# Three edits in the expert layers of an attention and two-MoE kernel: row masks first, 116-partition loads cut in two, two loads freed from a wait

## The chip, the cores and the metric

One core of a Trainium2 chip. The metric is the device time of one execution in microseconds (us). The kernel before was timed three times: median 1523.1 us, from 1520.05 to 1523.97. One further execution was profiled; the rows below come from it.

## What is computed

Attention without softmax over 4 sequences of 2496 tokens, then two expert layers (MoE) on the 9984 rows that come out. Cut to what matters:

```python
scores = scale * z @ z.T                      # per sequence
x = u * (maximum(scores, 0) ** 2 @ v)         # 9984 x 256
# first layer: only rows with x @ w_skip > 0; one expert of 8 per row
xc = x[x @ w_skip > 0]
e_idx = argmax(xc @ w_gate)
y[e_idx == e] = gate_w * (maximum(xc @ w1[e], 0) @ w2[e])
out = x;  out[chosen] = xc + y
# second layer: all rows, logits = x @ w_gate + modality_bias[modality_id]
out2[e_idx == e] = gate_w * (maximum(x @ w1[e], 0) @ w2[e])
```

Everything is float32; a product is made of three matmuls of a high and a low part (hh, hl, ...).

## The kernel before, in words

Attention writes its rows, sorted by expert, into two lists in DRAM: `rows1` (rows that the first layer computes) and `rows2` (rows that go straight to the second layer). The class `Moe1` works through `rows1` in tiles of 348 rows, held as 116 partitions x 3 rows (`P1, G1 = 116, 3`); `Moe2` through `rows2` in tiles of 512 rows, 128 partitions x 4. One tile is one *turn* (`turn`, with the lists `PLAN` that say what is done after which step): eight `hidden(f)` steps ("h", 0 to 7), eight `out_part(f)` steps ("o", 0 to 7). Between them hooks are called in the written order; the order on every engine is the order of the program (`manual_schedule`).

What a turn of Moe1 does beside its matmuls:

- "next", at the start: SyncE (SP) reads the next tile's row and expert, loads its rows into `x_in` (`load_rows`, line 758) and the first weights into `w1raw` (line 667). "load w2" follows at ("h", 5). Loads wait in SP's queue, in order.
- "after", eleven times: the gating of the tile computed in the turn before, as a list of steps: `taken` (ScalarE copies the outputs out of PSUM, lines 896 and 897), `low(0)`, `low(1)` with `masks` (lines 933 to 938, six small VectorE operations; `counted` is lines 790 and 791), `logits_t`, `logits` (line 926 reads `x_cur`), `first` (FirstMax, lines 115 to 121), `sums`, `exp`, `rows(0)`, `rows(2)` with `close`, `ranks`. `close` also loads the turn's own rows a second time, into `x_cur`.
- "w2": ScalarE makes the high part of the second weights, GpSimd (POOL) the low part with `TENSOR_TENSOR` (line 678), two of them for each of four blocks. "w1": ScalarE and VectorE (line 680).
- `send`: POOL scatters the rows of the last tile into `rows2`, three indirect DMAs (line 694) with small touches between (line 716).

In the order of VectorE `masks` stands between `low(1)` and the third `hl` (line 783), which frees a PSUM buffer that `hidden` needs (`ps_h` has three).

Turns in order: one inside the tail of attention, two with rows that are known, a loop (line 1206) over the table's tiles, one behind the loop in which Moe2's first tile (`ra`, of the expert with most rows) is loaded, one with Moe2's second known tile (`rb`), then Moe2's own turns and loop (line 1235). A loop ends with a meeting of all engines (shown at line 1296). `ra` and `rb` are registers that SP loads; those two tiles are full of rows that attention itself has written, if the expert has so many, and rows past the end are dropped by index.

Tile, the layer that places waits, lets a load from `rows2` wait for all scatters to `rows2` that come before it in the program, unless they are declared independent.

Of the kernel before, what the change touches and what calls it, by code (L numbers as in the profile page):

```python
# [104 lines left out]
class FirstMax:  # L105


    def __init__(self, nc, pool, k, lg, P, n, tag):
        self.nc = nc
        sh = [P, n, E]  # L110
        t = lambda name, *sh: pool.tile([128, *sh], F32, name=name + tag)[:P]
        mx, self.df, self.hot = t("mx", n), t("df", n, E), t("hot", n, E)
        self.ex, self.sm = t("ex", n, E), t("sm", n)
        df, hot = self.df, self.hot
        nc.vector.tensor_reduce(mx, lg, axis=AX.X, op=ALU.max)
        nc.vector.tensor_tensor(df, lg, mx.unsqueeze(2).to_broadcast(sh), op=ALU.subtract)
        nc.vector.scalar_tensor_tensor(
            hot, df, 0.0, k.desc[:P].unsqueeze(1).to_broadcast(sh), op0=ALU.is_equal, op1=ALU.mult
        )
        nc.vector.tensor_reduce(mx, hot, axis=AX.X, op=ALU.max)  # L120
        nc.vector.tensor_tensor(hot, hot, mx.unsqueeze(2).to_broadcast(sh), op=ALU.is_equal)
# [69 lines left out]
class Attention:  # L191
# [148 lines left out]
    def tail(self, b, c):  # L340
# [76 lines left out]
        for g in range(4):  # L417
            yield
            for s, (lst, w) in enumerate(((self.rows1, RW), (self.rows2, C_B2))):
                scatter(self.tc, f"list{s}", lst, ix[:, s, g:g + 1], r[:, g, 0:w])  # L420
# [208 lines left out]
class Shared:  # L629
# [35 lines left out]
    def load(self, i, e):  # L665
        w = self.w[e:e + 1] if isinstance(e, int) else self.w[ds(e, 1)]
        self.nc.sync.dma_start(self.raw[i], w.rearrange("o p w -> p (o w)")[:, i * 2048:(i + 1) * 2048])
# [21 lines left out]
        return self.hi[1][f // 2][:, f % 2], self.lo[1][f // 2][:, f % 2]  # L689


def scatter(tc, key, out, ix, rows, loop=False):

    i = tc.nc.gpsimd.indirect_dma_start(  # L694
        out=out, out_offset=bass.IndirectOffsetOnAxis(ap=ix, axis=0), in_=rows, in_offset=None,
        bounds_check=out.shape[0] - 1, oob_is_err=False,
    )
    i = getattr(i, "ins", i)
    tc.add_to_no_dep_group(key, i)
    tc.declare_no_dep(i, group=key, across_iterations=loop, reason="each row is written once")  # L700


class Scatter:
# [22 lines left out]
    def group(self, out, rows, width, g):  # L726
        last = rows[:, g, width - 1:width]
        self.touch(self.spare, last, last)
        scatter(self.tc, self.key, out, self.ix[:self.P, g:g + 1], rows[:, g, 0:width], True)
# [7 lines left out]
class Moe:  # L737
# [17 lines left out]

    def load_rows(self, r, dst=None):
        src = self.rows[r:r + self.T] if isinstance(r, int) else self.rows[ds(r, self.T)]
        self.nc.sync.dma_start(self.x_in if dst is None else dst, src.rearrange("(p g) w -> p g w", g=self.G))

    def x_transposed(self, d, ps=None, x=None):  # L760

        nc = self.nc
        ps = (self.sh.ps_x.tile([128, 512], F32, name="m") if ps is None else ps)[:, :self.T]
        for g in range(self.G):
            nc.tensor.transpose(  # L765
                ps[:, g * self.P:(g + 1) * self.P], (self.x_in if x is None else x)[:, g, d * 128:(d + 1) * 128],
                self.k.ident[:self.P, :self.P],
            )
        nc.scalar.copy(self.xh[:, d], ps)  # L769
        nc.vector.tensor_tensor(self.xl[:, d], ps, self.xh[:, d].bitcast(F32), op=ALU.subtract)  # L770
# [35 lines left out]
    def turn(self, follow, after, hooks=None):  # L806

        nc, sh = self.nc, self.sh
        nxt = []

        def hook(what, *args):
            if what == "next":
                nxt.extend(follow())
                nxt[0].load_rows(nxt[2])
                sh.load(0, nxt[1])
            elif what == "after":
                next(after, None)
            elif what == "w2":
                sh.split(1, args[0], nc.gpsimd)
            elif what == "w1":  # L820
                sh.split(0, args[0], nc.vector)
            elif what == "x":
                nxt[0].x_transposed(args[0])
            elif what == "load w2":
                sh.load(1, nxt[1])
            else:
                what()

        plan = self.PLAN if hooks is None else hooks
        for h in plan["start"]:  # L830
            hook(*h)
        self.work({at: [lambda h=h: hook(*h) for h in hs] for at, hs in plan.items()})
        for _ in after:
            pass


class Moe1(Moe):
# [45 lines left out]
    def after(self, lim, current, ps=None, gate_first=True):  # L883

        nc, k, P, G, T = self.nc, self.k, self.P, self.G, self.T
        s, sh = self.p, self.sh
# [12 lines left out]
        def low(d):  # L899
            nc.vector.tensor_tensor(yl[:, d], y[:, d], yh[:, d].bitcast(F32), op=ALU.subtract)  # L900
# [74 lines left out]

        both = lambda *f: lambda: [i() for i in f]
        exp = lambda: gate["first"].exp()
        begin = [taken, lambda: low(0), both(lambda: low(1), masks), logits_t]
        if gate_first:
            steps = begin + [logits, first, sums, exp, lambda: rows(0), both(lambda: rows(2), close), ranks]  # L980
        else:
# [16 lines left out]
class Moe2(Moe):  # L998
# [12 lines left out]

    def __init__(self, sh, k, rows, out):
        super().__init__(sh, k, rows, C_B2, P2, G2)
        self.out = out

    def more(self, p):
        super().more(p, "2")
# [4 lines left out]
    def take_y(self):  # L1022

        self.y = self.sh.y + [self.sh.ps_m.tile([128, 2 * D], F32, name="m") for _ in range(2)]

    def x_transposed(self, d):
        if d == 0:
# [61 lines left out]
def forward_kernel(ctx, tc, zT, v, uT, wg, wg2, mod, bias, w, out, nb=B, mode="reg_based"):  # L1089
# [33 lines left out]
    m2 = Moe2(sh, k, rows2, out)  # L1123
    spare = lambda: sh.ps_m.tile([128, 512], F32, name="m")
    nc.gpsimd.memset(sh.x_in, 0.0)
    with ExitStack() as main:
        a = Attention(tc, sh, ctx, main, k, zT, v, uT, wg, rows1, rows2, carry, nb)
# [7 lines left out]
        known = const.tile([128, 2, E], F32, name="known")  # L1135
# [73 lines left out]
    m1.send()  # L1209
    load = lambda i, lo, hi: nc.values_load(plan.er[0:1, i:i + 1], engines=[SP], min_val=lo, max_val=hi)  # L1210
    e2, ra, rb = load(0, E, 2 * E - 1), load(1, 0, E * N - T2), load(2, 0, E * N - T2)
    m1.turn(lambda: (m2, e2, ra), m1.finish(n))

    m1.send()
# [85 lines left out]
```

## Time and profile before

| | us |
|---|---|
| median of 3 runs | 1523.1 (1520.05 to 1523.97) |
| profiled execution | 1526.42 |
| its span, first to last instruction | 1524.5 |
| TensorE busy | 1477.5 (97%) |
| VectorE / ScalarE / GpSimd busy | 1091.3 / 944.6 / 610.2 |
| granted TensorE clock, mean | 0.995 |

Attention takes the span's first 734 us, Moe1's turns run from there to about 1079, Moe2's to the end. A row of the timeline reads: start, duration, engine, line, operation, output<-input, shape, count, and in brackets the idle time of the engine before it with what ended that. In the views PE is TensorE, DVE VectorE, ACT ScalarE, SP SyncE; a q behind the name is the engine's queue. An indirect DMA on POOL shows the time that POOL spends on it, not the transfer.

### The profile page before, as it was taken

The page shows a single profiled execution, that of the slowest core. Times are in us where ns is not written, and L with a number is a line of the kernel's source. Part 1 is how long each engine was busy: PE and PEld are TensorE (multiplying, and loading weights), DVE is VectorE, ACT ScalarE, POOL GpSimd, SP SyncE. Part 2 cuts the span into 40 slices and gives each one's busy share as a digit, 9 for nine tenths or more (in the row PEclk, how much of TensorE's full clock was granted, in tenths as well). Part 3 has the DMA queues.
Part 4 walks back from the last instruction along what each step waited for, and adds up shares of the span by engine and source line. Part 5 has one row for each costly group of instructions (what it writes and reads, how often), then busy time and mean ns, then how long its engine had stood idle before and what let it go on. Part 6 is the DMA issues. An engine that isn't in the chain of part 4 may idle for free. (4 is left out here: it accounts for less than half of the span.)

```text
span 1524.5 us, 35306 instructions
## 1 busy us (share of the span) xinstructions
PE 1477.5 (97%) x11020; PEld 1271.9 (83%) x11020; DVE 1091.3 (72%) x2587; ACT 944.6 (62%) x1713; POOL 610.2 (40%) x865
## 2 busy tenths in 40 slices
PE   7999999999999999999899999998999999999998
PEld 5888888788887887888789899997888888888886
DVE  7788887888877888787787778886655555555553
ACT  7777777777777777676445555555455455455453
POOL 3022322233322232222455555655454454454454
PEclk9999999999999999999999999999999999999999
DMA  9011211112111140011245555554343433443440
GB/s 365 23 43 63 71 36 42 42 57 76 38 44 53 48 143 28 30 41 62 86 128 165 162 167 164 170 170 141 130 155 124 153 136 124 142 143 127 140 146 27
DMA packets 49701, 160.29 MB, mean 105 GB/s; under 512 B 13285, under 2 KB 15195, under 8 KB 40384
## 3 DMA queue, kind: packets, MB, share of 16 engines
q1 hardware_dynamic: 28720, 124.24, 25.2%
q0 software_dynamic: 20736, 34.71, 6.5%
q8 instruction: 61, 1.00, 0.3%
q14 instruction: 40, 0.33, 0.1%
q10 hardware_dynamic: 144, 0.02, 0.0%
HBM read 124.24 MB, written 46.55 MB: 112 GB/s over the span
## 5 line engine op out<-in xcount | busy, mean ns | idle before, releaser
L694 POOL DMA_INDIRECT rows<-r,ix x160 | 199.4, 1246 | 332.4 <-DVE xs L347 238.2
L334 PE MATMUL o<-ah,vh 64*128 64x512 f32 (+1 forms) x1560 | 311.3, 386 | 9.5 <-DVE xs L347 9.5
L334 PE MATMUL o<-al,vh 64*128 64x512 f32 (+1 forms) x1560 | 303.0, 383 | 0.0
L334 PE MATMUL o<-ah,vl 64*128 64x512 f32 (+1 forms) x1560 | 301.6, 383 | 0.0
L783 DVE SCALAR_TENSOR_TENSOR hl<-ph,hh 128x512 fp32r<-128x512 f32 (+1 forms) x288 | 179.8, 674 | 164.0 <-ACT hh L782 160.9
L678 POOL TENSOR_TENSOR w<-w2raw,w 128x256 fp32r<-128x256 f32 x282 | 199.3, 743 | 181.5 <-issue 161.3
L291 ACT ACTIVATE t<-s 128x1024 f32<-128x1024 f32 (+2 forms) x201 | 202.3, 1007 | 95.7 <-PE s L288 90.2
L305 DVE TENSOR_TENSOR al<-t,ah 128x1024 fp32r<-128x1024 f32 (+2 forms) x201 | 240.0, 1194 | 18.3 <-PE s L288 0.5
L782 ACT ACTIVATE hh<-ph 128x512 fp32r<-128x512 f32 (+1 forms) x288 | 155.9, 541 | 130.7 <-PE ph L780 120.5
L780 PE MATMUL ph<-mxh,zA 128*128 128x512 f32 (+1 forms) x576 | 211.6, 367 | 11.4 <-DVE mlg L926 5.6
L303 ACT ACTIVATE t<-t 128x1024 f32<-128x1024 f32 (+2 forms) x201 | 208.1, 1036 | 5.8
L304 DVE CAST ah<-t 128x1024 fp32r<-128x1024 f32 (+2 forms) x201 | 137.4, 684 | 102.8 <-ACT t L303 63.4
L780 PE MATMUL ph<-mxl,zA 128*128 128x512 f32 (+1 forms) x576 | 208.8, 363 | 0.8 <-DVE mxl L770 0.8
L780 PE MATMUL ph<-mxh,zB 128*128 128x512 f32 (+1 forms) x576 | 208.6, 362 | 0.0
L334 PEld LDWEIGHTS o<-ah,vh 64*128 64x128 f32 x1560 | 150.4, 185 | 45.7 <-DVE xs L347 17.0
L334 PEld LDWEIGHTS o<-al,vh 64*128 64x128 f32 x1560 | 150.3, 185 | 27.3
L334 PEld LDWEIGHTS o<-ah,vl 64*128 64x128 f32 x1560 | 146.7, 185 | 27.4
L769 ACT CAST mxh<-m 128x512 fp32r<-128x512 f32 (+1 forms) x72 | 37.9, 526 | 168.4 <-PE m L765 103.3
L780 PEld LDWEIGHTS ph<-mxh,zA 128*128 128x128 f32 x576 | 109.7, 190 | 27.8 <-DVE mlg L926 5.8
L881 PE MATMUL o<-hh,w 128*128 128x348 f32 x512 | 128.7, 334 | 0.0
L288 PE MATMUL s<-zA,zB 64*128 64x512 f32 (+1 forms) x400 | 124.5, 389 | 0.0
L288 PE MATMUL s<-zB,zA 64*128 64x512 f32 (+1 forms) x400 | 122.1, 389 | 0.0
(236 smaller groups left out, 3070.9 us busy)
## 6 DMA issues: line engine op xcount, KB each, us to landing
w1raw<-in_w SPq DMA_DIRECT2D x36, 1024.0 KB, 6.7
w2raw<-in_w SPq DMA_DIRECT2D x36, 1024.0 KB
x_in<-rows SPq DMA_DIRECT2D x20, 520.0 KB
vraw<-in_v SPq DMA_DIRECT2D x20, 512.0 KB
ut<-in_uT SPq DMA_DIRECT2D x20, 512.0 KB
x_cur<-rows SPq DMA_DIRECT2D x16, 364.3 KB
x_in<-rows SPq DMA_DIRECT2D x15, 364.3 KB
rows<-x_in POOLq DMA_DIRECT2D x8, 536.0 KB
```

Source lines behind the costliest of these rows:

```text
L288: nc.tensor.matmul(s[:, i, :n], w[p, k], x[p, q], start=(j == 0), stop=(j == 2))
L291: nc.scalar.activation(t[:, i, :n], s[:, i, :n], AF.Relu, scale=SCALE)
L303: nc.scalar.activation(t[:, i, :n], t[:, i, :n], AF.Square)
L304: nc.vector.tensor_copy(h[:, i, :n], t[:, i, :n])
L305: nc.vector.tensor_tensor(l[:, i, :n], t[:, i, :n], h[:, i, :n].bitcast(F32), op=ALU.subtract)
L334: nc.tensor.matmul(o[half][d][:, :n], w[p, d * 128:d * 128 + 128], x[p, :n], start=(u == 0 and j == at[0]), stop=(u == 9 and j == at[-1]),)
L678: lo_engine.tensor_tensor(l[:, c], src[:, c], h[:, c].bitcast(F32), op=ALU.subtract)
L694: i = tc.nc.gpsimd.indirect_dma_start(out=out, out_offset=bass.IndirectOffsetOnAxis(ap=ix, axis=0), in_=rows, in_offset=None, bounds_check ...
L780: nc.tensor.matmul(ps, w, x, start=(i == 0), stop=(i == len(mms) - 1))
L782: nc.scalar.activation(h, ps, AF.Relu)
L783: nc.vector.scalar_tensor_tensor(l, ps, 0.0, h.bitcast(F32), op0=ALU.max, op1=ALU.subtract)
L881: nc.tensor.matmul(self.y[d], w[:, dd], h[f], start=(f == 0 and i == 0), stop=(f == 7 and i == 2))
```

## The change

1. `masks` leaves the third step of "after" and is put ahead of `taken` in the first, at the turn's start.
2. `load_rows` issues two transfers where the number of partitions isn't a multiple of 16: 112 partitions and 4 for Moe1's 116; Moe2's 128 stay one transfer. This goes for `x_in`, `x_two` and `x_cur`.
3. Moe2's loads of `ra` and `rb` are declared independent of the scatters of Moe1 ("scatter1"), and those scatters of the loads.

```diff
+def independent(tc, key, other, i, loop, reason):
+    tc.add_to_no_dep_group(key, i)
+    tc.declare_no_dep(i, group=other, across_iterations=loop, reason=reason)
 def scatter(tc, key, out, ix, rows, loop=False):
     i = getattr(i, "ins", i)
-    tc.add_to_no_dep_group(key, i)
-    tc.declare_no_dep(i, group=key, across_iterations=loop, reason="each row is written once")
+    independent(tc, key, key, i, loop, "each row is written once")
+    if loop:
+        tc.declare_no_dep(i, group="loads2", across_iterations=True, reason="rows behind those of full tiles")
 ...
     def load_rows(self, r, dst=None):
         src = self.rows[r:r + self.T] if isinstance(r, int) else self.rows[ds(r, self.T)]
-        self.nc.sync.dma_start(self.x_in if dst is None else dst, src.rearrange("(p g) w -> p g w", g=self.G))
+        dst = self.x_in if dst is None else dst
+        src = src.rearrange("(p g) w -> p g w", g=self.G)
+        most = self.P // 16 * 16
+        return [
+            self.nc.sync.dma_start(dst[p], src[p]).ins
+            for p in (slice(0, most), slice(most, self.P)) if p.start < p.stop
+        ]
 ...
-        begin = [taken, lambda: low(0), both(lambda: low(1), masks), logits_t]
+        begin = [both(masks, taken), lambda: low(0), lambda: low(1), logits_t]
 ...                                   # class Moe2
-        self.out = out
+        self.out, self.known = out, ()
+    def load_rows(self, r, dst=None):
+        for i in super().load_rows(r, dst):
+            if any(r is known for known in self.known):
+                independent(self.tc, "loads2", "scatter1", i, True, "a full tile's rows are there, others are dropped")
 ...                                   # forward_kernel, behind the first loop
+    m2.known = ra, rb
```

## Rows read from the trace of the kernel before

**Rows 1.** The page, part 1: busy time and share of the span, instructions.
```profile
PE 1477.5 (97%) x11020; PEld 1271.9 (83%) x11020; DVE 1091.3 (72%) x2587; ACT 944.6 (62%) x1713; POOL 610.2 (40%) x865
```

**Rows 2.** Waits of TensorE, whole span: us in total, times, longest.
```profile
PE ph L780 <- DVE mlg L926: 5.6, 2, 3.0
...
PE ph L780 <- PEq L1296: 2.6, 2, 1.9
PE m L956 <- DVE x_out L917: 2.0, 2, 1.7
PE ph L780 <- DVE hl L783: 1.6, 6, 0.3
PE m L765 <- DMA x_in<-rows: 1.6, 1, 1.6
```

**Rows 3.** Windows from one turn's first copy (line 896) to the next's; clock behind POOL.
```profile
839.29:857.98 18.69, 18.34 (x123) 17.62 (x122) 15.37 (x46) 10.66 (x24) 11.17 (x18) 1.00 0.57 169
857.98:881.72 23.74, 20.74 (x123) 20.30 (x122) 17.25 (x46) 10.67 (x24) 12.22 (x19) 0.86 0.46 138
...
937.04:955.02 17.98, 17.98 (x123) 17.63 (x122) 14.40 (x46) 10.67 (x25) 11.36 (x18) 1.00 0.58 179
...
801.28:821.31 20.03, 18.32 (x121) 17.58 (x122) 16.18 (x46) 10.88 (x24) 12.09 (x21) 1.00 0.54 155
778.57:801.28 22.71, 20.04 (x124) 19.30 (x122) 16.37 (x46) 10.67 (x25) 10.08 (x14) 0.92 0.52 159
```

**Rows 4.** Windows just behind the two longest waits; granted clock behind POOL's count.
```profile
787.70:791.10 3.40, 3.40 (x13) 3.40 (x13) 1.00 (x3) 0.97 (x2) 0.85 (x2) 0.50 0.28 101
...
866.20:873.00 6.80, 5.82 (x20) 5.82 (x21) 3.72 (x16) 1.47 (x4) 2.41 (x5) 0.50 0.06 20
```

**Rows 5.** Timeline of VectorE at the begin of the turn at 857.98.
```profile
856.64 1.29 DVE L680 TENSOR_TENSOR zB<-w1raw,zA 128x512 fp32r<-128x512 f32 x2
859.89 0.52 DVE L783 SCALAR_TENSOR_TENSOR hl<-ph,hh 128x348 fp32r<-128x348 f32 x1 [1.96 <-ACT hh L782]
...
862.37 4.70 DVE L936 TENSOR_SCALAR mk_drop<-mk 116x3 f32<-116x3 f32 x1
```

**Rows 6.** Timeline of GpSimd in the same stretch.
```profile
857.29 1.80 POOL L694 DMA_INDIRECT rows<-x_out,ix_scatter  x1 [0.53 <-issue]
...
861.34 1.54 POOL L694 DMA_INDIRECT rows<-x_out,ix_scatter  x1 [0.19 <-issue]
862.90 4.15 POOL L678 TENSOR_TENSOR w<-w2raw,w 128x256 fp32r<-128x256 f32 x6
```

**Rows 7.** Timeline of VectorE, the masks of another turn (at 881.72), first and last.
```profile
885.40 0.16 DVE L934 COPY limits<-lim 128x2 f32 x1
...
886.23 0.06 DVE L938 MEMSET cumb<- 116x4 uint32 x1
```

**Rows 8.** Line 936 and tile dfb: duration in ns, least/median/most, of all turns.
```profile
L936 DVE TENSOR_SCALAR mk_drop<-mk x16: 169/637/4703, 764.5 to 1057.8; 116x3 f32<-116x3 f32 x16
...
L116 DVE TENSOR_TENSOR dfb<-mlg,mxb x16: 182/706/2334, 768.2 to 1066.9; 116x24 f32<-116x24 f32 x16
```

**Rows 9.** Windows with one load alone (`x_cur`, then Moe2's `x_in`); last columns DMA share, GB/s.
```profile
1025.90:1029.40 3.50, 3.46 (x23) 3.15 (x21) 2.95 (x9) 1.49 (x3) 0.00 (x0) 1.00 0.24 86
1042.00:1043.50 1.50, 0.80 (x7) 0.52 (x5) 1.40 (x6) 0.01 (x1) 1.11 (x3) 1.00 0.98 329
```

**Rows 10.** Waits of SP's queue from 1024 to 1034: total, times, longest.
```profile
SPq L758 <- DMA rows<-x_out,ix_scatter: 7.3, 1, 7.3
...
SPq L1206 <- DMA x_cur<-rows: 1.5, 1, 1.5
```

**Rows 11.** Timeline of TensorE where the first loop ends.
```profile
1031.28 0.40 PE L780 MATMUL ph<-mxh,zA 128*128 128x348 f32 x1 [1.92 <-PEq L1296]
```

**Rows 12.** Timeline of SP: the loads behind the loop's last turn.
```profile
1024.84 0.30 SPq L758 DMA_DIRECT2D x_cur<-rows  x1
1040.58 0.35 SPq L758 DMA_DIRECT2D x_in<-rows  x1
```

## The prediction, made before the kernel was run

> **What bounds the kernel now.** I began with the page's busy shares: TensorE is busy 97% of the span [rows 1]. So only what shortens TensorE's 47 us of idle time, or speeds its matmuls, can pay. The next view is who TensorE waited for [rows 2]. Five of its waits lie in the stage that the change touches: 5.6 us for `mlg` in two waits, the longer 3.0; 2.6 us in two meetings at loop ends, the longer 1.9, so 0.7 for the other; 2.0 us for `x_out`, most of it one wait of 1.7; 1.6 us for `hl`, six waits of about 0.27; and 1.6 us for one `x_in` load. Together 13.4 us. The rest of the list lies in attention or in the hand-over to it.
>
> The third view cuts Moe1's stage into turns [rows 3]. It shows more than the waits do. Undisturbed turns take 17.98 us (the loop has four, 17.96 to 17.98); the six with the short `hl` wait take 18.7 (five of them 18.66 to 18.71, the sixth is the loop's last); the turns with the long `mlg` waits take 23.74 and 22.71, the first loop turn 20.03. In the two longest, the granted clock means 0.86 and 0.92 instead of 1.00. The fourth view looks just behind their waits: clock 0.50, that is 1.2 instead of 2.4 GHz, for 6.8 us and 3.4 us, after TensorE had stood idle for 3.0 and 2.6 us [rows 4]. So a long wait is paid twice.
>
> Why does `mlg` come late? Not for its data: in the slow turn VectorE is inside `mk_drop`, a 116x3 operation, for 4.70 us [rows 5]. In other turns it takes 0.17 us; the median is 0.64 [rows 8]. It starts at 862.37, while GpSimd works on a scatter (861.34, 1.54 us), and ends at 867.07, as GpSimd's six back-to-back subtractions end (862.90 + 4.15 = 867.05) [rows 6]. VectorE is in order, so three `hl` and `mlg` stand behind it. I read this as one shared way to SBUF which VectorE loses to GpSimd several times in a row.
>
> **Part 1, masks first.** It removes six small VectorE operations from between `low(1)` and the third `hl` and puts them behind the last `zB` of the turn before. No instruction is added. What goes, against the profiled execution (1526.42 us):
> - The turn at 857.98: 23.74 - 17.98 = 5.8 us [rows 3].
> - The turn at 778.57 isn't of the loop's form, so I take its wait and its clock: 5.6 - 3.0 = 2.6 us of waiting [rows 2], and 3.4 us at half the clock, which cost 1.7 [rows 4]. Together 4.3.
> - Six turns at 18.7: at most 18.69 - 17.98 = 0.7 each, 4.2 together [rows 3]; at least the 1.6 us of waits for `hl` [rows 2]. The difference of turns counts all of it, but the later `dfb` may keep a part: I take 0.6 each, 3.6.
> - The first loop turn, 20.03 - 17.98 = 2.05 us [rows 3], is a hold of `dfb` (2.33 us, its longest) by the same GpSimd subtractions [rows 8]. `dfb` isn't moved: I take 0, with 2.05 as the other end.
>
> What it costs: unheld, the six take 885.40 to 886.29, so 0.9 us [rows 7]. At the turn's start VectorE stands idle 1.96 us before the first `hl`, waiting for ScalarE [rows 5]; that covers them. If that cover is gone, the first `hl` is late. At that time GpSimd is on its first scatter: 857.29 + 1.80 = 859.09 [rows 6]. Masks held until then end at 859.09 + 0.9 = 859.99, against 859.89 for `hl` [rows 5], 0.1 us late. I take 0. The other end is a TensorE wait as for today's late `hl`, 0.27 us in each of some 14 turns, 3.8 us [rows 2]. `taken` is on ScalarE and isn't queued behind the masks. What is queued behind them on VectorE: the first `hl` and `low(0)`. POOL's scatters may be held by the masks in turn, by less than the 0.9 us.
>
> Here a page of the Trainium skill says something else. "SBUF — State Buffer", section "SBUF: two separate sides", states that VectorE and GpSimd share a pair of ports, which the one that starts first holds for its whole instruction while the other is blocked. By that rule a small operation waits for one instruction, not for six; the 4.70 us [rows 6] would need another cause, and the two long waits might stay. That is a rival below.
>
> **Part 2, loads in two.** The 116-partition load of `x_cur`, alone on the DMA engines, keeps 0.24 of the 16 busy, some four, at 86 GB/s; Moe2's 128-partition load 0.98 at 329 GB/s [rows 9]. So 112 partitions should go over many more engines, and land sooner. In the loop no TensorE wait names `x_cur`, and the `x_in` wait is behind the loop [rows 2]: no gain there. At the loop's end there is one: the meeting waits 1.5 us of SP's time for `x_cur` to land [rows 10], and TensorE stands idle 1.92 us [rows 11]. The meeting of Moe2's loop, where no such load is under way, costs 0.7 us [rows 2]: 1.9 - 0.7 = 1.2 us gained. The cost is one more issue of 0.3 us on SP per load [rows 12], moved ahead of the load of `w1raw`, for which no TensorE wait is seen [rows 2]; I take 0. Ends: a loss of 0.3 us in the one turn whose `x_in` is waited for, and no gain at all.
>
> The skill has a rule against this edit: "DMA: Bandwidth & Descriptors", section "Rules for kernel authors", says not to bother with two transfers to separate partitions, since both run over the same 16 engines. Its section "Why a DMA increments its semaphore by 16 and not by 1" has the number of engines as the largest divisor up to 16, which is 4 for 116 and 16 for 112; the trace's 0.24 agrees with that one. By the first alone the 1.2 us would not come.
>
> **Part 3, known tiles.** Behind the loop SP waits 7.3 us for scatters [rows 10] before it issues `x_in` at 1040.58 [rows 12]; TensorE then waits 1.6 us for it [rows 2]. Issued 7 us sooner, the load is hidden: 1.6 us gained. `w1raw` stands behind it in SP's queue and comes sooner too. For `rb` no TensorE wait is seen: 0. The end below is that it collides with scatters; I know no row that prices that above the 1.6.
>
> **Sum.** 5.8 + 4.3 + 3.6 + 1.2 + 1.6 = 16.5 us; 1526.4 - 16.5 = 1509.9 in a profiled execution. That execution is 3.3 us above the median of the runs shown. Either profiling costs that, or it met a long hold that the median run missed (one is worth 4.3 to 5.8). I take half, 1.5 us: **1508.5 us**. With all upper ends (4.2 for 3.6, 2.05 for 0, 3.3 for 1.5) it is 1504; with the lower ends (1.6 for 3.6, late `hl` 3.8, a loss of 0.3 for the gain of 1.2) 1515.7.
>
> **Rivals.**
> - *The holds move.* `dfb`, with two SBUF inputs, stays in GpSimd's stream. The shift in phase lets it be held in more turns, at 2.05 us each. For: it happened once in 16, and phases decide. Against: its median is 0.7 us. Four turns: 16.5 - 8.2 = 8.3 gained, 1516.5.
> - *The long holds stay or weren't in the timed runs.* `mk_drop` then waits for something other than the subtractions, which comes along to its new place, or the median run has no long hold to lose. The page's rule above points to the first. Left are 3.6 + 1.2 + 1.6 = 6.4 from the median: 1516.7. Against: both long holds are on `mk_drop`.
> - *The loads don't do what they should*, neither faster nor freed: 2.8 less, 1511.3.
> - *Slower.* The masks at the start hold the scatters' descriptors, GpSimd's subtractions start late in every turn as in the first loop turn, and `dfb` is held each time: 13 x 2.05 = 26.7, less 16.5: 10 us slower, 1535. It decides from 8 turns on (16.5 / 2.05). Against: one turn of 16 does it.
>
> **Chances.** Forecast 0.56, moved holds 0.16, long holds stay 0.13, loads do nothing 0.08, slower 0.07. The range 1503 to 1519 leaves out the slower case and the tails of the second and third, under 0.2. A difference under 0.3% (4.6 us) can't be told from none. Faster by more: 0.56 + 0.08 + 0.12 + 0.08 = 0.84; within: 0.09; slower 0.07.
>
> **What would show it.** Right: `mk_drop` nowhere over about 1 us and ahead of the first `hl`; no wait for `mlg`; all loop turns near 18.0; clock 1.00 in them; the first loop's meeting near 0.7; DMA share near 1 for Moe1's loads; `x_in` behind the loop issued some 7 us sooner, with no TensorE wait. Wrong: `dfb` or another small operation with times over 2 us in several turns, the first `hl` late at the turns' start, or a clock of 0.50 in a new place.

## The result, and the profile of the changed kernel

| | before | changed |
|---|---|---|
| median of 5 runs each, same chip | 1522.75 us (1520.05 to 1523.97) | 1508.45 us (1507.55 to 1509.91) |
| ratio, 95% interval | | 0.9909 (0.9898 to 0.9921) |
| profiled execution, time | 1526.42 us | 1509.91 us |
| profiled execution, span | 1524.5 us | 1507.8 us |

The change saves 14.3 us in the medians and 16.5 us between the two profiled executions. It was forecast at 1508.5 us, from a sum of 16.5 us.

The page of the changed kernel, part 1 (engine, busy us, share of the span, instructions), has the same counts as [rows 1]. The work is the same, and TensorE's share rises from 97% to 98%:

```profile
PE 1471.7 (98%) x11020; PEld 1268.7 (84%) x11020; DVE 1082.8 (72%) x2587; ACT 949.7 (63%) x1713; POOL 614.7 (41%) x865
```

Waits of TensorE over the whole span of the changed kernel (us in total, times, longest). The new lines 969, 793, 930 and 1315 are 956, 780, 917 and 1296 of before:

```profile
PE m L969 <- DVE x_out L930: 3.8, 4, 1.6
PE m L154 <- DVE cuma L140: 2.5, 1, 2.5
...
PE ph L793 <- PEq L1315: 1.4, 2, 0.7
```

Against [rows 2], `mlg` (5.6), `hl` (1.6) and `x_in` (1.6) are gone from the list, and the two meetings are 0.7 each. `x_out` has grown from 2.0 to 3.8.

Windows of the changed kernel: the second turn with known rows ("the second turn" from here on), the loop's first turn, its third, an ordinary one, its fourth, which took 23.74 before, the turn behind the loop, and a stretch in the turn inside attention's tail. Columns: length, busy time of TensorE, its weight loads, VectorE, ScalarE and GpSimd, granted clock, DMA share, GB/s:

```profile
778.70:797.05 18.35, 18.32 (x124) 17.67 (x122) 14.19 (x44) 10.59 (x24) 9.83 (x14) 1.00 0.60 192
797.05:817.00 19.95, 18.29 (x121) 17.64 (x122) 15.95 (x46) 10.84 (x24) 11.88 (x21) 1.00 0.49 161
834.99:852.94 17.95, 17.95 (x123) 17.58 (x122) 14.15 (x47) 10.65 (x24) 11.16 (x18) 1.00 0.55 175
852.94:871.91 18.97, 18.20 (x123) 17.56 (x122) 15.18 (x47) 10.77 (x24) 11.43 (x18) 1.00 0.52 168
1016.60:1036.55 19.95, 18.41 (x122) 17.67 (x123) 15.15 (x47) 10.97 (x24) 12.20 (x21) 1.00 0.57 182
750.50:757.30 6.80, 6.50 (x29) 6.21 (x30) 6.29 (x28) 0.66 (x2) 0.72 (x1) 0.50 0.62 219
```

The second turn falls from 22.71 to 18.35. The turn that took 23.74, the loop's fourth, falls to 18.97 and not to an undisturbed 17.95: its long hold is gone, but another operation is now held in it (below). Five of the six turns at 18.7 are at 17.95; the sixth, the last loop turn, takes 18.99 with the meeting in it (20.92 before). The loop's twelve turns together fall from 230.02 to 219.55 us. In these turns the clock is 1.00; the two half-clock stretches of [rows 4] are gone. The only one left in this stage lies ahead of them, in the turn inside attention's tail, behind the 2.5 us wait for `cuma`. There it lasts 6.8 us; in the kernel before a wait of 3.2 us for `cuma` was followed by 3.4 us of it. The turn behind that one, the first with known rows, is 0.3 us longer (19.41 to 19.71).

Two groups of VectorE in the changed kernel, duration in ns (least/median/most) over all turns:

```profile
L949 DVE TENSOR_SCALAR mk_drop<-mk x16: 169/373/503, 760.2 to 1037.9; 116x3 f32<-116x3 f32 x16
...
L116 DVE TENSOR_TENSOR dfb<-mlg,mxb x16: 182/184/2306, 767.8 to 1051.3; 116x24 f32<-116x24 f32 x16
```

Against [rows 8], `mk_drop`'s longest falls from 4703 to 503 ns. `dfb` still has a longest of 2.3 us, and now three turns have such a hold: 2.31 us in the first loop turn (as before), 1.93 in the loop's fourth turn, at 852.94, and 2.10 in the one behind the loop. The turn at 852.94 shows what holds it. VectorE first, then GpSimd, each as start, duration, line, operation, tiles:

```profile
861.58 1.93 DVE L116 TENSOR_TENSOR dfb<-mlg,mxb 116x24 f32<-116x24 f32 x1
```

```profile
856.21 1.62 POOL L700 DMA_INDIRECT rows<-x_out,ix_scatter  x1 [0.19 <-issue]
857.86 5.60 POOL L678 TENSOR_TENSOR w<-w2raw,w 128x256 fp32r<-128x256 f32 x8
```

`dfb` ends at 863.51, the subtractions at 863.46: the picture of [rows 5] and [rows 6] with another victim.

But not every small operation in the stream is held. The loop's third turn, an ordinary one, VectorE and then GpSimd:

```profile
843.62 0.18 DVE L116 TENSOR_TENSOR dfb<-mlg,mxb 116x24 f32<-116x24 f32 x1
```

```profile
838.07 1.26 POOL L700 DMA_INDIRECT rows<-x_out,ix_scatter  x1 [0.18 <-issue]
839.50 5.63 POOL L678 TENSOR_TENSOR w<-w2raw,w 128x256 fp32r<-128x256 f32 x8 [0.17 <-issue]
```

Here the subtractions run from 839.50 to 845.13, and `dfb` passes among them in its least time. What lets an operation pass isn't shown; the two turns differ in when the subtractions start, 4.5 and 4.9 us behind the turn's begin.

The masks in their new place, VectorE at an ordinary turn's start in the changed kernel:

```profile
942.33 1.28 DVE L680 TENSOR_TENSOR zB<-w1raw,zA 128x512 fp32r<-128x512 f32 x2
943.57 0.06 DVE L946 MEMSET mk_drop<- 116x3 f32 x1
...
944.67 0.06 DVE L951 MEMSET cumb<- 116x4 uint32 x1
945.65 0.52 DVE L796 SCALAR_TENSOR_TENSOR hl<-ph,hh 128x348 fp32r<-128x348 f32 x1 [0.92 <-ACT hh L795]
```

Six operations take 1.2 us from first to last (0.9 unheld [rows 7]), and 0.92 us of VectorE's idle time is left behind them: the cover was enough.

The loop's end in the changed kernel: TensorE at the meeting, then SP's issues behind it, then a window with the load of `x_cur` alone (last columns: clock, DMA share, GB/s):

```profile
1016.57 0.40 PE L793 MATMUL ph<-mxh,zA 128*128 128x348 f32 x1 [0.73 <-PEq L1315]
```

```profile
1018.68 0.36 SPq L769 DMA_DIRECT2D x_in<-rows  x1
1019.28 0.35 SPq L667 DMA_DIRECT2D w1raw<-in_w  x1
```

```profile
1012.30:1013.50 1.20, 1.20 (x11) 1.18 (x10) 1.02 (x6) 0.40 (x2) 0.00 (x0) 1.00 0.81 298
```

The meeting's wait falls from 1.92 [rows 11] to 0.73. `x_in` is issued 2.1 us behind the meeting's matmul instead of 9.3 [rows 11, 12]. The DMA share of the load rises from 0.24 to 0.81 [rows 9].

### The profile page after: what moved, and what is told of

Its sections match the earlier page's. It is cut to its first block, busy times and chain, and to the rows that moved or that the text cites. A ratio compares the mean times of both kernels' runs of the same rounds, so it can differ in the third digit from the quotient of the medians.

```text
span 1507.8 us, 35395 instructions
## 1 busy us (share of the span) xinstructions
PE 1471.7 (98%) x11020; PEld 1268.7 (84%) x11020; DVE 1082.8 (72%) x2587; ACT 949.7 (63%) x1713; POOL 614.7 (41%) x865
## 5 line engine op out<-in xcount | busy, mean ns | idle before, releaser
L700 POOL DMA_INDIRECT rows<-r,ix x160 | 205.5, 1285 | 339.0 <-DVE xs L347 244.5
L796 DVE SCALAR_TENSOR_TENSOR hl<-ph,hh 128x512 fp32r<-128x512 f32 (+1 forms) x288 | 176.5, 614 | 156.7 <-ACT hh L795 156.0
L793 PEld LDWEIGHTS ph<-mxh,zA 128*128 128x128 f32 x576 | 108.4, 188 | 19.6 <-issue 3.7
```

Source lines behind the costliest of these rows:

```text
L700: i = tc.nc.gpsimd.indirect_dma_start(out=out, out_offset=bass.IndirectOffsetOnAxis(ap=ix, axis=0), in_=rows, in_offset=None, bounds_check ...
L793: nc.tensor.matmul(ps, w, x, start=(i == 0), stop=(i == len(mms) - 1))
L796: nc.vector.scalar_tensor_tensor(l, ps, 0.0, h.bitcast(F32), op0=ALU.max, op1=ALU.subtract)
```

## The experiments

The theory has three parts. A VectorE operation is held by GpSimd's stream of subtractions for as long as that runs; 116 partitions go over four DMA engines; and SP waits needlessly behind the loop. The rivals: the masks wait for something else, the holds only move, and the loads are no faster in two transfers.

### The parts alone

**Part 1 alone**, on the kernel before:

```diff
-        begin = [taken, lambda: low(0), both(lambda: low(1), masks), logits_t]
+        begin = [both(masks, taken), lambda: low(0), lambda: low(1), logits_t]
```

> Part 1 alone: the kernel before with the masks at the turn's start, loads and waits as before. Theory (the parts add up, masks carry the gain): 16.5 - 1.2 - 1.6 = 13.7 us of the profiled difference, so about 1510 to 1512 timed; no mk_drop over 1 us, no TensorE wait for mlg; the first loop's meeting still about 1.9 us and the x_in wait still about 1.6 us. Rival (the faster loads took the holds away, by changing the phases): 1517 or more, with long holds left.

Measured: 1513.6 us against 1524.1 for before on the same chip, ratio 0.9937 (0.9921 to 0.9954). That is 10.5 us, less than expected. Its tile `dfb` (ns, least/median/most) and its waits of TensorE:

```profile
L116 DVE TENSOR_TENSOR dfb<-mlg,mxb x16: 182/188/2306, 766.9 to 1055.3; 116x24 f32<-116x24 f32 x16
```

```profile
PE m L956 <- DVE x_out L917: 4.9, 5, 1.6
...
PE ph L780 <- PEq L1296: 3.4, 2, 2.7
```

No wait for `mlg` is left, and `mk_drop` takes at most 0.50 us. But in five turns, four more than before, `dfb` takes 1.9 to 2.3 us: the loop's first (19.96 us), three others of the loop, which take 18.9 to 19.0, and the one behind it. And the meeting at the loop's end waits 2.7 us instead of 1.9: TensorE arrives sooner, the load of `x_cur` doesn't. So the rival of moved holds is real, at about 1 us a turn in the loop, and part 2 is worth more behind part 1 than alone.

**Part 2 alone**: `load_rows` as in the change, the rest as before.

```diff
-        self.nc.sync.dma_start(self.x_in if dst is None else dst, src.rearrange("(p g) w -> p g w", g=self.G))
+        dst = self.x_in if dst is None else dst
+        src = src.rearrange("(p g) w -> p g w", g=self.G)
+        most = self.P // 16 * 16
+        return [
+            self.nc.sync.dma_start(dst[p], src[p]).ins
+            for p in (slice(0, most), slice(most, self.P)) if p.start < p.stop
+        ]
```

> Part 2 alone: loads of 112 and 4 partitions, masks and waits as before. Theory: 1.2 us less (1521 to 1522, not to be told from before), the meeting of the first loop at about 0.7 us, DMA share near 1 instead of 0.24 where x_cur loads alone; mk_drop still with holds over 2 us, mlg waits still there. Rival (loads are the cause of the holds): 1515 or less. Rival (two transfers run over the same few engines): meeting 1.9 us, share 0.25.

Measured: 1522.52 against 1524.07, 0.9987 (0.9978 to 0.9997). TensorE at the loop's end and behind it, in part 2 alone:

```profile
1027.55 0.40 PE L786 MATMUL ph<-mxh,zA 128*128 128x348 f32 x1 [0.73 <-PEq L1302]
...
1040.61 0.63 PE L771 MATMUL m<-ident,x_in 128*128 128x128 f32 x4 [1.42 <-DMA x_in<-rows]
```

The meeting is at 0.73, the wait for `x_in` behind the loop stays, and so do both waits for `mlg` (5.6 us) and both half-clock stretches. The faster load gives the meeting's 1.2 us and leaves the holds alone.

**Part 3 alone**: `independent` and `known` as in the change, loads in one transfer, masks in their old place.

```diff
 ...                                   # `independent`, `scatter` and class Moe2 as in the change
+    m2.known = ra, rb
```

> Part 3 alone: known tiles don't wait for scatters, masks and loads as before. Theory: 1.6 us less (about 1521, not to be told from before), the x_in load behind the first loop issued some 7 us sooner and no TensorE wait for it. Rival (the load then collides with the scatters or waits for something else): the wait stays at 1 us or more.

Measured: 1522.67 against 1524.07, 0.9992 (0.9979 to 1.0005): not told from no change. The profiled execution took 1519.86, 2.8 us less than the median, so its trace shows what part 3 can meet and doesn't account for the median. TensorE in the second turn and at the loop's end:

```profile
788.37 0.49 PE L772 MATMUL m<-ident,x_in 116*128 116x116 f32 x3 [1.59 <-DMA x_in<-rows]
...
1025.49 0.40 PE L787 MATMUL ph<-mxh,zA 128*128 128x348 f32 x1 [3.13 <-PEq L1309]
```

`x_in` behind the loop is issued at 1027.59 without waiting for scatters, and no TensorE wait for it is left. But a 116-partition load is waited for in the second turn, 1.59 us, where in this execution `mk_drop` is held for 1.67 us only; and the meeting waits 3.13 us, followed by 3.4 us at half the clock. SP waits 2.7 us for `x_cur` there, against the 1.5 of [rows 10], though the load is issued at the same place in the turn (14.44 us behind its begin, 14.46 before); why it lands later isn't shown. In this execution these losses, some 4.5 us (1.6, 1.2 and 1.7), are more than the 1.6 that part 3 saves. In parts 2 and 3 together, below, the wait in the second turn is gone and the meeting is at 0.7.

**Parts 2 and 3**: the changed kernel with the masks put back.

```diff
-        begin = [both(masks, taken), lambda: low(0), lambda: low(1), logits_t]
+        begin = [taken, lambda: low(0), both(lambda: low(1), masks), logits_t]
```

> The changed kernel with part 1 undone: masks behind low(1) again. Theory: 2.8 us less than before, 1519 to 1521; one to three mk_drop over 2 us, clock 0.50 behind the waits that reach some 2.5 us. Rival (parts 2 and 3 carry more than their waits): under 1515.

Measured: 1519.7 against 1524.07, 0.9972 (0.9962 to 0.9982), 4.4 us: inside the expected 1519 to 1521. With part 1's 10.5 that is 14.9, near the 14.3 of the whole. In the profiled execution the tile `mk_drop` still has its long hold, one in place of two:

```profile
L949 DVE TENSOR_SCALAR mk_drop<-mk x16: 169/599/4698, 764.1 to 1048.9; 116x3 f32<-116x3 f32 x16
```

In the second turn it is missing (0.17 us, where the kernel before has 4.37). So the 4.4 us may hold something of a long hold that this phase happened to miss, and can't be taken as the price of parts 2 and 3 by themselves. The turn behind the loop takes 19.12 us here, with no wait for `x_in` and no hold of `dfb`, against 20.83 before.

### The cause of the holds

**No subtractions on GpSimd**: the kernel before, in which Moe1's turns on the usual plan (no hooks of their own: the second turn, the loop, the one behind it) leave out GpSimd's subtractions. The low part of `w2` isn't renewed there; all else runs.

```diff
-                sh.split(1, args[0], nc.gpsimd)
+                sh.split(1, args[0], None if hooks is None and self.P == P1 else nc.gpsimd)
 ...                                   # in split, behind ScalarE's copy
+        if lo_engine is None:
+            return
```

> The kernel before without GpSimd's subtractions in Moe1's turns from the third on (the low part of the second weights isn't renewed there, so those rows come out less exact); masks in the old place. Theory: no mk_drop and no dfb over 0.8 us, no mlg wait, loop turns near 18.0 us, clock 1.00 in the loop; 12 to 16 us less than before (1507 to 1511). Rival (the hold is from the scatters' descriptors or from data): holds of 2 us and more stay, 1517 or more.

Measured: 1513.59 against 1523.14, 0.9947 (0.9930 to 0.9964). The tiles `mk_drop` and `dfb`, ns:

```profile
L938 DVE TENSOR_SCALAR mk_drop<-mk x16: 168/169/172, 762.4 to 1042.5; 116x3 f32<-116x3 f32 x16
```

```profile
L116 DVE TENSOR_TENSOR dfb<-mlg,mxb x16: 182/183/521, 765.9 to 1051.6; 116x24 f32<-116x24 f32 x16
```

```profile
PE m L767 <- DMA x_in<-rows: 4.5, 2, 2.3
```

With the masks in their old place and the scatters as they were, `mk_drop` takes 0.17 us in every turn, nothing waits for `mlg`, and the loop's turns take 17.95, but for the first (18.14) and the last (19.65, with the meeting). So the turns without the subtractions have no holds; the scatters alone make none. One thing stays open: in [rows 5] and [rows 6] `mk_drop` starts 0.53 us ahead of the first subtraction, longer than its 0.17 us, and what holds it until then isn't shown. The time missed the expected 1507 to 1511. Two waits for `x_in` take 4.5 us: one of 2.2 in the second turn, with 3.4 us at half the clock behind it, came up where the hold had hidden a slow load; the one behind the loop grew from 1.6 to 2.3.

**The masks in the middle of the stream**: the changed kernel with the masks one step later than in the kernel before.

```diff
-        begin = [both(masks, taken), lambda: low(0), lambda: low(1), logits_t]
+        begin = [taken, lambda: low(0), lambda: low(1), both(masks, logits_t)]
```

> The changed kernel with the masks one step later than in the kernel before, beside logits_t, in the middle of GpSimd's subtractions. Theory (GpSimd's stream holds VectorE's small operations): each of four operations is held up to 0.7 us, some for several subtractions; masks take 2 to 5 us in a turn instead of 0.9, hl behind them late, TensorE waits 1 us or more in most of 14 turns: 1520 or more. Rival (mk_drop was held by something that belongs to its place before the scatter's end or to its data): masks take about 0.9 us, 1508 to 1511.

Measured: 1527.89 against 1523.14, 1.0032 (1.0019 to 1.0045): 4.7 us slower than before in spite of parts 2 and 3, and 19 us behind the changed kernel (timed on another chip). Its waits of TensorE, and the first copy of the masks (ns, least/median/most):

```profile
PE ph L793 <- DVE hl L796: 12.3, 4, 4.3
```

```profile
L947 DVE COPY limits<-lim x14: 160/161/5664, 800.5 to 1062.1; 128x2 f32 x14
```

A copy of two numbers per partition, 0.16 us alone, takes up to 5.66 us; `mk_hi` up to 5.67. Three turns take 23 to 26 us, each with a half-clock stretch. In the other loop turns three mask operations take 0.6 to 0.7 us each. So the place of the masks decides, and in both directions.

### The rule of the loads

**Two halves**: the changed kernel with 58 + 58 partitions in place of 112 + 4.

```diff
-        most = self.P // 16 * 16
+        most = self.P if self.P % 16 == 0 else self.P // 2
```

> The changed kernel with loads of 58 and 58 partitions instead of 112 and 4. Theory (the number of engines is the largest divisor up to 16, here 2 for each): DMA share at most 0.25 in a lone x_cur load, the first loop's meeting at 1.9 us or more, 1509.5 to 1512. Rival (two transfers in flight are what makes it faster): share about 0.5 or more, meeting near 0.7, 1508 to 1509.

Measured: 1577.82 against 1523.14, 1.0358 (1.0342 to 1.0373). The direction was expected, the size by no means: 1509.5 to 1512 had been written. Its waits of TensorE, and a window with `x_cur` alone:

```profile
PE m L778 <- DMA x_in<-rows: 50.5, 13, 8.6
```

```profile
1076.50:1083.50 7.00, 4.33 (x29) 4.03 (x27) 2.68 (x6) 1.49 (x3) 0.00 (x0) 1.00 0.13 51
```

A share of 0.13 is two engines of 16 for both halves together, with 51 GB/s: the second transfer, issued 0.4 us behind the first, adds none to the first's two. Whether it goes over the same two or waits for them isn't shown. The load of `x_in` no longer fits into a turn, and TensorE waits for it in 13 turns. Against the changed kernel, timed on another chip, 69 us are lost: 50.5 here, 3.4 at the meeting (4.1 in place of 0.7), and the rest, some 15, goes with a mean granted clock of 0.982 in place of 0.997. My expectation priced the loads by the meeting alone and didn't ask when they cease to be hidden.

### The holds that are left

**Ranks' rows first**: the changed kernel, `after` with `gate_first=False` in Moe1's loop and in the turn behind it, so that the gate's steps (with `dfb`) come behind the copies of rows.

```diff
-        return self.after(table.lim[:, :, ds(j + self.table.S - 1, 1)], lambda: table.row(self.nc, j, self.T))
+        return self.after(
+            table.lim[:, :, ds(j + self.table.S - 1, 1)], lambda: table.row(self.nc, j, self.T), None, False
+        )
```

> The changed kernel with the order that its last Moe1 turn has also in the loop and the turn behind it: rows(0) and rows(2) before the logits, so that dfb and the other small operations with two SBUF inputs run when GpSimd's subtractions are over. Theory: no dfb over 0.8 us in those turns, TensorE's waits for x_out (3.8 us in four) down to one of 0.9, 1504 to 1507. Rival (the small operations, now later, make the ranks and so the scatters late, or rows wait for the last scatter of x_out): new TensorE waits, 1509 or more.

Measured: 1529.88 against 1523.14, 1.0047 (1.0033 to 1.0061). Its waits of TensorE:

```profile
PE m L969 <- DVE ohbb L959: 8.2, 12, 0.7
PE m L937 <- DVE x_out L930: 4.7, 2, 3.3
...
PE m L970 <- DVE cumb L963: 2.0, 12, 0.2
```

The holds of `dfb` are gone but for one of 1.7 us in the second turn, and the rival took their place: the ranks come before their chain on VectorE is ready, in eleven of the loop's turns, ten of which take 19.4 to 19.6 us (the last 20.5, with the meeting). The loop's first turn takes 24.5, with the wait of 3.3 us for `x_out` and 6.8 us at half the clock; the turn behind the loop takes 22.1.

**The gate late, the ranks last**: the changed kernel with another order of the steps in all of Moe1's turns but the last.

```diff
-            steps = begin + [logits, first, sums, exp, lambda: rows(0), both(lambda: rows(2), close), ranks]
+            steps = begin + [logits, lambda: rows(0), lambda: rows(2), both(first, exp), sums, close, ranks]
```

> The changed kernel with the gating's steps in another order: logits, rows(0), rows(2), first and exp, sums, close, ranks, with ranks in the old place (it came one step earlier in the run with rows first). dfb and the other small operations then stand at ('h', 7), when GpSimd's subtractions are over in an ordinary turn, and a step is left between sums and ranks. Theory: no dfb over 1 us in the loop's ordinary turns, TensorE's waits for x_out (3.8 us in four) and for ohbb (8.2 us in the run with rows first) both under 2 us in total: 1504 to 1507. Rival (the chain from first to ranks is too short of time at its late place, as in the run with rows first): a wait for ohbb or cumb in most turns, 1510 or more.

**The changed kernel again**, on the same chip:

> The changed kernel itself beside the run before, on the same chip. 1507 to 1510; dfb held for about 2 us in two to four turns, wherever GpSimd's subtractions start 4.9 us or more after the turn's begin, and in none where they start before 4.7.

Measured against 1521.93 for before: the late gate 1507.76 (1505.76 to 1508.74), 0.9899 (0.9880 to 0.9917); the changed kernel 1509.62 (1507.95 to 1511.99), 0.9911 (0.9894 to 0.9928). The late gate is just above the 1504 to 1507 that I had expected. Its waits of TensorE that answer to the `x_out` wait, and its tile `dfb`:

```profile
PE m L969 <- DVE ohbb L959: 0.5, 1, 0.5
PE m L970 <- DVE cumb L963: 0.3, 2, 0.2
```

```profile
L116 DVE TENSOR_TENSOR dfb<-mlg,mxb x16: 182/182/523, 770.8 to 1049.6; 116x24 f32<-116x24 f32 x16
```

No hold is left and the 3.8 us for `x_out` are 0.8 for the ranks. In the medians it is 1.9 us ahead of the changed kernel, but the intervals overlap: the trace shows the gain, the times don't tell the two apart.

The repeated run of the changed kernel has its holds of `dfb` in the same three turns, 2.30, 1.94 and 2.07 us. GpSimd's subtractions start there 6.2, 4.9 and 6.1 us behind the turn's begin; in the other turns on the usual plan they start at 4.4 to 4.6, and `dfb` isn't held. So it is the phase of a turn that decides, not chance. In the loop's fourth turn the late start isn't made by the change: in the kernel before, too, they start 4.9 us behind its begin [rows 6], and it was `mk_drop` that was held. There the last scatter ahead of them takes longer, 1.62 us in the changed kernel against 1.26 in the turn before it. Why it does, and why they start later still in the other two turns, stays open.

## Why the prediction was right, and where it was not

- **The long holds, 5.8 and 4.3.** Right in the mechanism: both holds are gone, and their half clock with them. The second turn lost 4.36 us (22.71 to 18.35), as forecast. The loop's fourth turn lost 4.77 (23.74 to 18.97) and not 5.8, since `dfb` is now held in it. The cause, a stream of subtractions rather than one, is shown from both sides: without the stream there is no hold, and with the masks put into it the holds grow to 5.7 us. That the stream holds an operation for as long as it runs, as the theory above has it, is too strong: most small operations in it are held for no longer than about one subtraction (0.7 us) or pass, by the phase. Here the row and the Trainium skill differ ("SBUF — State Buffer", "SBUF: two separate sides"): it has the second engine blocked until the first one's instruction is done, and `mk_drop` sat through six [rows 6]. The measurement decides.
- **Six short turns, 3.6.** Each came back whole, about 0.74, 4.4 together: the upper end of 4.2 would have been the better value.
- **Masks at nothing.** Right: 0.92 us of idle time is left behind them. No wait for `hl` is left.
- **`dfb` at nothing.** Half right. The first loop turn keeps its hold (20.03 to 19.95), but two turns more are held, which comes near the prediction's sign of being wrong (over 2 us in several turns): they cost 1.0 us in the loop's fourth (18.97 against 17.95), and 0.8 in the turn behind the loop (19.95 against the 19.12 of parts 2 and 3, where `dfb` isn't held there). The rival of moved holds, with four turns of 2.05, came true in two turns, at half the price or less. With part 1 alone it came true in four, so the other two parts took some of these away; by what path was not settled.
- **The meeting, 1.2.** Right, 1.92 to 0.73. The DMA share of the load reached 0.81, not quite the forecast's near 1. What I didn't see: with part 1 alone the wait grows to 2.7, with part 3 alone to 3.1. The two transfers are worth more in company than by the sum. The Trainium skill's advice against two transfers to disjoint partition halves ("DMA: Bandwidth & Descriptors", "Rules for kernel authors") can't be carried over to 112 + 4 partitions (share 0.24 to 0.81); for 58 + 58, which are halves, it holds (0.13).
- **Known tiles, 1.6.** Right: the wait is gone, and it stays in part 2 alone, so it is part 3 that removes it. With parts 2 and 3 that turn is 1.7 us shorter (20.83 to 19.12). In the changed kernel it is only 0.9 shorter (19.95), since `dfb` is now held there for 2.10 us.
- **The sum.** 16.5 was measured as 16.5 between the profiled executions. The turns that the sum names gave 4.8 + 4.4 + 4.4 + 1.2 + 0.9 = 15.7: the short turns made up for part of what the new holds took. Some 1.1 us of the rest lie behind this stage, where the sum has nothing. That the two agree to 0.1 is partly luck.
- **The offset of 1.5.** A guess that came out by luck. The profiled execution of before lies 3.7 us above the median of its five runs, that of the changed kernel 1.5 above its own. The medians therefore differ by 14.3, not 16.5, and the forecast of 1508.5 meets the median of 1508.45. No fixed price of profiling is seen: the changed kernel's second profiled execution lies 2.4 us above its median, that of part 3 alone 2.8 below.

## What to carry to other kernels

Look for small VectorE operations that last several times their least, and see what GpSimd is running then: put them where GpSimd isn't in a row of tensor operations, into idle time that VectorE has anyway. A transfer whose partition count isn't a multiple of 16 (116 here) deserves a look at its DMA share; splitting off the remainder mended it here, splitting in halves made it worse. When a wait is removed, list what it had been hiding: the slow load of the second turn came up as soon as the hold in it went.

## What the runs showed of the hardware that was not expected

- A copy of 128x2 numbers on VectorE, begun during a scatter just ahead of GpSimd's stream of eight subtractions, took 5.66 us, against 0.16 alone; it ended among the subtractions.
- Waits of 2.5 us (`cuma`) and 3.1 us (the meeting in part 3 alone) were followed by 6.8 and 3.4 us at a granted clock of 0.50, that is 1.2 GHz: the longer wait had the shorter stretch behind it.
- Two transfers of 58 partitions kept 0.13 of the DMA engines busy, less than the 0.24 of a single one of 116.
